# Attention and two expert layers on one core: blocks of 512 tokens, first batch in plain fp32, other planner costs

## The chip, the cores and the metric

One core of a Trainium2 chip. The metric is the device time of one execution in microseconds; lower is better.

## The reference

Attention over 4 batches of 8 heads with 576 positions of width 64, where only scores within `tau` of a row's maximum count, and then two layers, each a product up to width 2048, an activation and a product back, over the 2304 tokens of width 512, all in fp32:

```python
scores = scale * np.matmul(q, k.transpose(0, 1, 3, 2))
thresh = np.max(scores, axis=-1, keepdims=True) - tau
scores = np.where(scores >= thresh, scores, -1000000000.0)
attn = softmax(scores)
x = np.matmul(attn, v)            # then transposed to (2304, 512)
...
h = x @ w_in                      # (512, 2048)
g = np.where(h > 0.0, h, np.exp(np.minimum(h, 0.0)) - 1.0)
x = g @ w_out                     # (2048, 512)
...
h = x @ w_in2
g = np.maximum(0.01 * h, h)
out = g @ w_out2
```

## The kernel before

**Number format.** A product of two fp32 matrices is made of three products in the faster fp32r format (line 630, `passes`): high by high, high by low, low by high parts. Splitting a matrix into its parts takes a rounding copy (`copy` on ScalarE or `hi_of`) and a subtraction (`tt`). [...]

**Attention.** A unit is 128 query rows by 576 keys; 9 units make a pair of heads, 36 a batch, 144 all. In `unit` (line 423) TensorE forms the scores, for heads below `Q32` in plain fp32 from 64 partitions (`qk32`, line 456), for the others from split parts (`qk`, line 463); VectorE takes the maximum (line 475), VectorE or GpSimd adds the threshold (478, 480), ScalarE masks (484) and exponentiates (487), VectorE inverts the sum (489), GpSimd or ScalarE normalizes (490), TensorE transposes (499, 514). `weights` (520) copies the transposed weights out of PSUM: for heads below `P32` with plain copies on ScalarE only (534, 536), for the others as split parts. `pv32` (575) and `pv` (593) form the product with v. `head` (377) loads a head's k, q and v; for heads from `Q32` on, GpSimd splits k and q in four instructions (410 to 415) after two DMAs for each of k and q (404 to 409); for heads below it one DMA each (394, 395).

**Layers beside the attention.** The layers work hidden tile by hidden tile, 128 of the 2048 at a time: `step_h` (633) forms h and its activation, and two steps later (`LAG`) `step_y` (676) adds the tile's part to y in PSUM. A step has 12 matmuls of each. While the attention goes on, six blocks of `TA` = 256 tokens do the first 8 of 16 hidden tiles of layer 1; the partial y goes to memory (`evac_a`, 723). The weights are read as 64-bit numbers and turned to fp32 in seven instructions on several engines (`weight`, 249).

**Past the attention**, from about 484 us on, blocks of `TB` = 384 tokens: two finish the first 8 tiles of layer 1 for the tokens left, six do the other 8 tiles of layer 1 (`evac_b`, 743, adds the partial y), six do the 16 tiles of layer 2 (`evac_c`, 753, writes the output in four DMAs a block). h has two PSUM banks, y four.

**The order of the work.** `Order` (88) plays the whole kernel through before it is emitted: each operation has a list of engines it may run on, a duration, dependencies and a due time `vt`; whichever engine is free first takes the operation that is due first, and each engine's program is the order that comes out (108 to 176). On the chip each engine then runs its program strictly in that order. The durations are formulas (179 to 208), such as a matmul of n columns and a DMA issue on SP (60 ns, as in line 255); due times come from the unit's number times `TU` and from offsets per step (`KN`, `ST0`, `ST1`, lines 42 to 48).

Of the kernel before, what the change touches and what calls it, by code (L numbers as in the profile page):

```python
# [20 lines left out]
NH = B * H  # L21
NU = 9
# [3 lines left out]
KC = DM // 128  # L26
FC = DFF // 128
FH = FC // 2
TA, TB = 256, 384
NB = NT // TB  # L30
# [14 lines left out]
ST0 = dict(qk=3991.2, max=-10812.2, thr=3582.6, exp=-4547.6, mask=9303.1, rec=4415.0, norm=-40669.8, tr=-20834.8,  # L45
           hi=-16434.5, lo=-12049.7, lhi=-1872.6, llo=30507.0, pv=-26126.1)
ST1 = dict(qk=-8436.2, max=5560.8, thr=-5954.0, exp=-1392.3, mask=-1204.3, rec=3126.6, norm=3036.1, tr=1924.8,
           hi=-17963.2, lo=-6188.5, lhi=-3977.0, llo=993.8, pv=-5778.3)
PE, ACT, DVE, POOL, SP, HOST = "PE", "ACT", "DVE", "POOL", "SP", "HOST"

# [37 lines left out]
class Order:  # L88
# [19 lines left out]
    def run(self):  # L108
# [9 lines left out]
        free = dict.fromkeys(engines, 0.0)  # L118
# [84 lines left out]
def mm(n):  # L203
    return 3 + n / 2.4
# [7 lines left out]
def attn_moe_kernel(ctx, tc, qT, kT, vm, tau, w1i, w1o, w2i, w2o, yp, out):  # L212
# [145 lines left out]

    op((PE, 2200 + 1450 * KN["warm"], warm), [], [wps], -1e6)

    heads = {}

    def load_tau(vt):
# [9 lines left out]
        ld = op((SP, 60, lambda: nc.sync.dma_start(out=taut, in_=tau.partition_broadcast(128))), [], [], vt - 2e4,  # L373
# [3 lines left out]
    def head(g, u):  # L377
        vt = (u - KN["hleadb" if g % 2 else "hlead"]) * TU
        par = g % 2
        if g < P32:  # L380
            v = v_r.new(F32)
            ov = op((SP, 60, lambda: nc.sync.dma_start(out=v()[:, :, 0:D], in_=vm[g])), [], [v], vt + KN["vlate"],
                    lat=3000)
        else:
            vr, v = vraw_r.new(), v_r.new()
            hi, lo = (lambda: v()[:, :, 0:D]), (lambda: v()[:, :, D:2 * D])
            lv = op((SP, 60, lambda: nc.sync.dma_start(out=vr(), in_=vm[g])), [], [vr], vt - 3000, lat=3000)
# [3 lines left out]
        if g < Q32:  # L391
            k, q = k1_r.new(F32), k2_r.new(F32)
            due = vt - (3e3 if g else 3e4)
            lk = op((SP, 60, lambda: nc.sync.dma_start(out=k()[0:64], in_=kT[g])), [], [k], due, lat=3000)
            lq = op((SP, 60, lambda: nc.sync.dma_start(out=q()[0:64, 0:S], in_=qT[g])), [], [q], due, lat=3000)
# [12 lines left out]
        lk = op((SP, 120, lambda: load2(kr, kT)), [], [kr], vt - 3000, lat=3000)  # L408
        lq = op((SP, 120, lambda: load2(qr, qT)), [], [qr], vt - 3000, lat=3000)
# [333 lines left out]
    def evac_b(i, tb, ybank, ysl, last, xc, vt):  # L743
        ys = ysb[i]
        x1[i] = []
        for m in range(KC):
            yg = ybank[m][0]
            o = op((DVE, dve(TB), lambda m=m, yg=yg: nc.vector.tensor_tensor(
                out=x[:, m, i * TB:(i + 1) * TB], in0=yg(), in1=ys[0]()[:, m, :], op=ALU.add)),
                [last[m], ys[1], xc[m][2]], [yg, ys[0]], vt)  # L750
            x1[i].append([o])

    def evac_c(i, tb, ybank, ysl, last, xc, vt):
        for m in range(KC):
            yg = ybank[m][0]
            dst = x[:, m, i * TB:(i + 1) * TB]
            o = op([(ACT, actp(TB), lambda yg=yg, dst=dst: nc.scalar.copy(out=dst, in_=yg())),
                    (DVE, dve(TB), lambda yg=yg, dst=dst: nc.vector.tensor_copy(dst, yg()))],
                   [last[m], xc[m][2]], [yg], vt)
            op((SP, 60, lambda m=m, dst=dst: nc.sync.dma_start(  # L760
                out=out[m * 128:(m + 1) * 128, i * TB:(i + 1) * TB], in_=dst)), [o], [], vt, lat=2000)
# [18 lines left out]
    def block_deps(i, tb):  # L780
        b0, b1 = i * tb // S, ((i + 1) * tb - 1) // S
# [18 lines left out]
    DT = 24 * mm(TB)  # L800
# [8 lines left out]
    TT = TE + len(rest) * FH * DT  # L809
    for i in range(NB):  # L810
        vt0 = TT + i * FH * DT
        ys = ys_r.new()
        ysb[i] = (ys, op((SP, 60, lambda ys=ys, i=i: nc.sync.dma_start(out=ys(), in_=yp[:, :, i * TB:(i + 1) * TB])),
                         [o for (lo, hi), o in ypdone.items() if lo < (i + 1) * TB and hi > i * TB], [ys], vt0,
                         lat=4000))
        block(0, i, list(range(FH, FC)), TB, block_deps(i, TB)[0], hps_b, yps_b, evac_b, vt0, DT)
    T2 = TT + NB * FH * DT
# [53 lines left out]
```

## Time and profile before

| | us |
|---|---|
| median of 3 runs | 1154.95 |
| lowest, highest | 1151.43, 1155.05 |
| the profiled execution | 1155.41 |
| its span, first to last instruction | 1153.6 |
| TensorE busy (share of the span) | 1110.1 (96%) |
| VectorE, ScalarE, GpSimd busy | 706.3, 684.9, 437.7 |
| mean granted clock of TensorE | 0.984 |

PE is TensorE's matmuls, PEld its weight loads, DVE VectorE, ACT ScalarE, POOL GpSimd, SP the engine that issues all DMAs. L686 is line 686 of the kernel. A matmul's own duration has its modelled end in it, and so busy times of PE overlap; the chain of waits counts from one release to the next. The granted clock is a share of 2.4 GHz: 1.00 is that, 0.50 is 1.2 GHz.

### The profile page before, as it was taken

To read this page: it belongs to the slowest core of one execution; us is meant where nothing else is said; L and a number is where in the kernel's file an instruction comes from. 1 tells how busy PE (TensorE), PEld (TensorE's weight loads), DVE (VectorE), ACT (ScalarE), POOL (GpSimd) and SP (SyncE) were. 2 spreads that over 40 slices of the span, in tenths; PEclk is the share of its full clock that TensorE was granted. 3 is DMA by queue.
4 is the path that set the end of the run, shared out by engine and by line. 5 is a ranking of instruction groups with operands and counts; after the bars stand their busy time and mean duration, and the time that the engine had idled before them with its cause. 6 is when DMAs were issued, how large, how long until landed. Compare 5 with 4: busy or idle time off the path is not lost.

```text
span 1153.6 us, 18990 instructions
## 1 busy us (share of the span) xinstructions
PE 1110.1 (96%) x6888; PEld 1045.8 (91%) x6888; DVE 706.3 (61%) x1629; ACT 684.9 (59%) x1488; POOL 437.7 (38%) x544
## 2 busy tenths in 40 slices
PE   6988889999999999999999999999999999999998
PEld 3555469998999999999999999999999999999998
DVE  3555678877888888688988744884323233232322
ACT  4899998999999999655555533553323232232321
POOL 4577588888889978422222100120000000000000
PEclk7899899999999999999999999999999999999999
DMA  6343312122222212134543300430000000000000
GB/s 153 88 124 109 93 56 56 52 77 74 62 69 61 74 56 65 38 96 133 165 137 119 119 14 20 132 111 19 28 1 28 1 1 28 1 28 1 28 1 28
DMA packets 39437, 73.47 MB, mean 64 GB/s; under 512 B 10033, under 2 KB 23217, under 8 KB 39345
## 3 DMA queue, kind: packets, MB, share of 16 engines
q1 hardware_dynamic: 39344, 72.27, 21.2%
q8 instruction: 54, 0.88, 0.3%
q14 instruction: 39, 0.31, 0.1%
HBM read 62.82 MB, written 9.44 MB: 63 GB/s over the span
## 4 chain that ended last, share of the span: by engine, by line
PE 73%; ACT 14%; DVE 6%; POOL 3%; issue 2%; DMA 1%; SPq 0%; POOLq 0%; ACTq 0%; DVEq 0%
PE y L686 32%; PE h L645 17%; PE hb L645 14%; ACT e L487 4%; ACT ss L484 3%; PE t L499 2%; PE v L604 2%; PE s L467 2%; ACT wh L544 2%; PE v L585 2%; DVE ss L475 2%; ACT e L304 1%; DVE wl L547 1%; DVE tm L567 1%; ACT wh L566 1%
## 5 line engine op out<-in xcount | busy, mean ns | idle before, releaser
L686 PE MATMUL y<-gh,woh 128*128 128x384 f32 (+1 forms) x832 | 270.1, 325 | 0.8 <-DVE ys L567 0.8
L686 PE MATMUL y<-gl,woh 128*128 128x384 f32 (+1 forms) x832 | 268.0, 322 | 0.0
L686 PE MATMUL y<-gh,wol 128*128 128x384 f32 (+1 forms) x832 | 267.9, 322 | 0.0
L645 PE MATMUL h<-xh,wih 128*128 128x384 f32 (+1 forms) x512 | 165.6, 324 | 0.8 <-DVE g L663 0.7
L645 PE MATMUL h<-xh,wil 128*128 128x384 f32 (+1 forms) x512 | 161.0, 314 | 0.0
L645 PE MATMUL h<-xl,wih 128*128 128x384 f32 (+1 forms) x512 | 161.0, 314 | 0.0
L686 PEld LDWEIGHTS y<-gh,woh 128*128 128x128 f32 x832 | 156.6, 188 | 1.0 <-DVE ys L567 1.0
L686 PEld LDWEIGHTS y<-gl,woh 128*128 128x128 f32 x832 | 156.6, 188 | 0.1
L686 PEld LDWEIGHTS y<-gh,wol 128*128 128x128 f32 x832 | 156.6, 188 | 0.0
L670 ACT CAST gh<-g 128x384 fp32r<-128x384 f32 (+1 forms) x208 | 101.6, 489 | 90.3 <-DVE g L668 49.6
L298 POOL TENSOR_TENSOR xl<-x,xh 128x256 fp32r<-128x256 f32 (+1 forms) x35 | 30.1, 875 | 280.3 <-ACT xh L623 280.0
L297 DVE TENSOR_TENSOR gl<-g,gh 128x384 fp32r<-128x384 f32 x151 | 86.5, 574 | 57.4 <-ACT gh L670 57.3
L475 DVE TENSOR_SCALAR_CACHE_REDUCE ss<-s,scl 128x576 f32<-128x576 f32 x124 | 100.5, 811 | 22.8 <-ACT e L487 17.5
L484 ACT ACTIVATE ss<-ss,thr 128x576 f32<-128x576 f32 x144 | 111.1, 775 | 3.6 <-POOL thr L478 2.1
L487 ACT ACTIVATE e<-ss,taun 128x577 f32<-128x577 f32 x144 | 112.0, 778 | 0.8
L467 PE MATMUL s<-k,qt 128*128 128x288 f32 x528 | 97.3, 306 | 11.0 <-DVE ss L475 6.7
L645 PE MATMUL hb<-xh,wih 128*128 128x384 f32 x320 | 106.9, 334 | 0.0
L645 PE MATMUL hb<-xl,wih 128*128 128x384 f32 x320 | 106.9, 334 | 0.0
L645 PE MATMUL hb<-xh,wil 128*128 128x384 f32 x320 | 106.9, 334 | 0.0
L645 PEld LDWEIGHTS h<-xh,wih 128*128 128x128 f32 x512 | 96.8, 189 | 2.2 <-DVE g L663 2.1
L499 PE MATMUL t<-ident,e 128*128 128x128 f32 x576 | 90.1, 281 | 7.1 <-ACT e L304 3.8
L645 PEld LDWEIGHTS h<-xl,wih 128*128 128x128 f32 x512 | 96.6, 189 | 0.0
(536 smaller groups left out, 2204.2 us busy)
## 6 DMA issues: line engine op xcount, KB each, us to landing
kraw<-in_kT_dram SPq DMA_DIRECT2D x60, 160.0 KB, 2.9
qraw<-in_qT_dram SPq DMA_DIRECT2D x60, 144.0 KB, 2.8
wraw<-in_w1i_dram SPq DMA_DIRECT2D x16, 512.0 KB, 3.7
wraw<-in_w1o_dram SPq DMA_DIRECT2D x16, 512.0 KB, 3.7
wraw<-in_w2i_dram SPq DMA_DIRECT2D x16, 512.0 KB, 3.6
wraw<-in_w2o_dram SPq DMA_DIRECT2D x16, 512.0 KB, 3.6
ys<-yp_dram SPq DMA_DIRECT2D x6, 768.0 KB, 4.7
out_dram<-x SPq DMA_DIRECT2D x24, 192.0 KB, 1.9
```

The lines of the kernel that those rows point to most:

```text
L297: return pick(who, D=(dve(n), lambda: nc.vector.tensor_tensor(**args()), PORT), P=(pool_tt(n), lambda: nc.gpsimd.tensor_tensor(**args())))
L298: P=(pool_tt(n), lambda: nc.gpsimd.tensor_tensor(**args())))
L467: nc.tensor.matmul(s()[:, j, 0:HALF], q()[:, c:c + 128], kk()[:, k0 + j * HALF:k0 + (j + 1) * HALF], start=(n == 0 and m == 0), stop=(n == ...
L475: o = op((DVE, dve(S) + 60, lambda: nc.vector.tensor_scalar(out=ssr().rearrange("p (j c) -> p j c", j=2), in0=s()[:, :, 0:HALF], scalar1=s ...
L484: o = op((ACT, act(S) + 95, lambda: nc.scalar.activation(out=ssr(), in_=ssr(), func=AF.Prelu, bias=thr(), scale=-1.0, alpha=STEEP)), [ot], ...
L487: o = op((ACT, act(S) + 190, lambda: nc.scalar.activation(out=er(S + 1), in_=ssr(S + 1), func=AF.Exp, bias=taun, accum_out=su())), [o], [s ...
L499: nc.tensor.transpose(t4()[:, c, :], er()[:, c1 + c * 128:c1 + (c + 1) * 128], ident)
L544: nc.scalar.copy(out=wh()[:, :, dst], in_=t4()[:, :, src])
L585: nc.tensor.matmul(ps()[0:64, 0:nw], lhs, rhs, start=(c == 0), stop=(c == 4))
L645: nc.tensor.matmul(hp(), w_()[:, cs], x_()[:, 0:tb], start=(k == 0 and z == 0), stop=(k == KC - 1 and z == 2))
L670: o1 = op((ACT, act(tb), lambda: nc.scalar.copy(out=gh()[:, cs], in_=g()[:, cs])), [o], [g, gh], vt)
L686: nc.tensor.matmul(ysl(yg, m), w_()[:, cs], g_()[:, 0:tb], start=(first and z == 0 and share == 0), stop=(last and z == 2 and end))
```

## The change

`TB` becomes 512. The blocks past the attention are no longer numbered but listed by their first token and length: four of 512 and one of 256 (for the tokens left by the attention stage: one of 512 and one of 256). `Q32` goes from 2 to 8, so that all heads of the first batch have k and q in plain fp32. The copies of transposed weights of heads below `P32` may go to ScalarE or VectorE. The planner takes 600 ns for a DMA issue on SP (1200 for a pair), 13.3 ns instead of 3 ns as a matmul's fixed part, and a time at which each engine begins. The due times are other numbers. The DMA scratch area in SBUF shrinks to 1024 bytes.

```diff
-TA, TB = 256, 384
-NB = NT // TB
+TA, TB = 256, 512
+BLOCKS = [(a, min(TB, NT - a)) for a in range(0, NT, TB)]
...
-Q32, P32 = 2, 9
+P32, Q32 = 9, 8
...
-KN = dict(warm=3, TU=2767.5, hlead=1.68307, hleadb=3.8618, wv0=2.81039, wv1=2.45697, yoff=29757.8, coff=-4793.0,
-          NS=41, vlate=3019.0, bs=[46.53, 62.85, 80.6, 98.984, 114.51, 129.21], bdt=1.99144, look=0.0937904)
+KN = dict(warm=3, TU=2691.9, hlead=0.875114, hleadb=3.14713, wv0=3.2304, wv1=2.45697, yoff=28639.7, coff=-5493.3,
+          NS=41, vlate=-1134.2, bs=[46.53, 62.85, 80.6, 98.984, 114.51, 134.31], bdt=1.98186, look=0.0900086)
...
+BEGIN = {PE: 2100.0, ACT: 2000.0, DVE: 2400.0, POOL: 1300.0, SP: 700.0}
...
-        free = dict.fromkeys(engines, 0.0)
+        free = {e: BEGIN.get(e, 0.0) for e in engines}
...
 def mm(n):
-    return 3 + n / 2.4
+    return 13.3 + n / 2.4
...
-        ld = op((SP, 60, lambda: nc.sync.dma_start(out=raw().rearrange("p c w -> p (c w)"), in_=src.bitcast(U32))),
+        ld = op((SP, 600, lambda: nc.sync.dma_start(out=raw().rearrange("p c w -> p (c w)"), in_=src.bitcast(U32))),
...
-    op((PE, 2200 + 1450 * KN["warm"], warm), [], [wps], -1e6)
+    op((PE, 1430 * KN["warm"], warm), [], [wps], -1e6)
...
-        lk = op((SP, 120, lambda: load2(kr, kT)), [], [kr], vt - 3000, lat=3000)
+        lk = op((SP, 1200, lambda: load2(kr, kT)), [], [kr], vt - 3000, lat=3000)
...
             if f32:
-                o1 = op(copy_of("A", 4 * n, lambda wh=wh, dst=dst: wh()[:, :, dst],
+                o1 = op(copy_of("AD", 4 * n, lambda wh=wh, dst=dst: wh()[:, :, dst],
                                 lambda src=src: t4()[:, :, src]), [ott], [t, wh], vt)
-                o3 = op(copy_of("A", n, lambda lt=lt, dst=dst: lt()[64:128, dst],
+                o3 = op(copy_of("AD", n, lambda lt=lt, dst=dst: lt()[64:128, dst],
                                 lambda src=src: lv()[l0:l0 + 64, src]), [otl], [lv, lt], vt)
...
-    rest = list(range(len(beside) * TA // TB, NB))
-    for n, i in enumerate(rest):
-        deps, _ = block_deps(i, TB)
-        block(0, i, list(range(FH)), TB, deps, hps_b, yps_b, evac_a, TE + n * FH * DT, DT)
+    vt = TE
+    for t0, tb in BLOCKS:
+        if t0 >= len(beside) * TA:
+            block(0, t0, list(range(FH)), tb, block_deps(t0, tb)[0], hps_b, yps_b, evac_a, vt, dt(tb))
+            vt += FH * dt(tb)
...
-    for i in range(NB):
-        block(1, i, list(range(FC)), TB, x1[i], hps_b, yps_b, evac_c, T2 + i * FC * DT, DT)
+    for t0, tb in BLOCKS:
+        block(1, t0, list(range(FC)), tb, x1[t0], hps_b, yps_b, evac_c, vt, dt(tb))
+        vt += FC * dt(tb)
...
-    nc = _bacc.Bacc("TRN2", target_bir_lowering=False, num_devices=1)
+    nc = _bacc.Bacc("TRN2", target_bir_lowering=False, num_devices=1, dynamic_dma_scratch_size=1024)
```

## Rows read from the trace of the kernel before

**Rows 1.** Windows: PE, PEld, DVE, ACT, POOL busy us (x count), clock, DMA share, GB/s.

```profile
36.00:168.00 132.00, 111.64 (x567) 70.56 (x566) 79.73 (x220) 125.43 (x267) 95.20 (x103) 0.96 0.35 96
168.00:484.00 316.00, 307.12 (x2419) 296.31 (x2420) 261.40 (x720) 292.66 (x707) 263.69 (x352) 1.00 0.21 59
484.00:1150.00 666.00, 665.99 (x3843) 665.67 (x3842) 350.47 (x646) 250.00 (x486) 63.16 (x69) 1.00 0.17 54
```

**Rows 2.** The chain of waits: start us, us, what; products are on L604, L645, L686.

```profile
88.70 2.46 PE v L585 x10
...
474.13 1.31 PE v L604 x9
475.45 1.44 PE h L645 x12
476.88 0.44 PE t L499 x4
...
490.63 2.08 PE y L686 x12
...
1148.46 2.12 DVE x L758 x4
```

**Rows 3.** Windows of line 484, the mask, one per unit: ScalarE's busy us (x masks).

```profile
36.00:140.00 104.00, 24.40 (x32) 0.95 0.39 107
```

**Rows 4.** Groups of ScalarE, 36 to 168 us: count | busy us, mean ns | idle before.

```profile
L566 ACT COPY wh<-t 128x512 f32<-128x512 f32 x33 | 19.3, 586 | 4.0 <-PE t L499 3.5
L304 ACT ACTIVATE e<-e,rs 128x576 f32<-128x576 f32 x22 | 17.0, 771 | 0.3 <-DVE rs L489 0.2
L566 ACT COPY lt<-h 64x128 f32<-64x128 f32 x34 | 8.8, 260 | 1.0 <-PE h L514 0.3
```

**Rows 5.** Groups of the whole span: VectorE's copy of 128x512 out of PSUM.

```profile
L567 DVE COPY ys<-y 128x512 f32<-128x512 f32 x7 | 4.8, 692 | 2.7 <-PE y L686 2.5
```

**Rows 6.** Windows of GpSimd's instructions on kraw (first row) and qraw (second).

```profile
36.00:168.00 132.00, 20.41 (x18) 0.96 0.35 96
...
36.00:168.00 132.00, 17.37 (x16) 0.96 0.35 96
```

**Rows 7.** TensorE's timeline at full clock: start us, us, engine, line, operation.

```profile
35.77 1.23 PE L460 MATMUL y<-k,k 64*128 64x288 f32 x4
36.93 0.66 PE L499 MATMUL t<-ident,e 128*128 128x128 f32 x4
...
106.31 2.37 PE L585 MATMUL v<-wh,v 128*64 128x320 f32 x8 [0.98 <-ACT wh L566]
...
109.29 0.66 PE L499 MATMUL t<-ident,e 128*128 128x128 f32 x4
...
110.43 0.69 PE L467 MATMUL y<-k,qt 128*128 128x288 f32 x4
110.96 0.60 PE L499 MATMUL t<-ident,e 128*128 128x128 f32 x4
```

**Rows 8.** The timeline of the start; in brackets the idle time and its releaser.

```profile
6.33 1.23 PE L460 MATMUL s<-k,k 64*128 64x288 f32 x4
...
10.97 0.69 DVE L280 CUSTOM_DVE_ANT_0 wb__144<-wb__144,wa__136 128x1024 uint16<-128x1024 uint16 x1 [0.73 <-ACT wa__136 L278]
...
11.58 0.81 DVE L475 TENSOR_SCALAR_CACHE_REDUCE ss<-s,scl 128x576 f32<-128x576 f32 x1
...
12.45 2.28 PE L460 MATMUL s<-k,k 64*128 64x288 f32 x4 [3.92 <-DVE ss L475]
...
17.19 0.67 POOL L302 TENSOR_SCALAR qt<-qraw 128x576 fp32r<-128x576 f32 x1 [3.53 <-DMA qraw<-in_qT_dram]
17.84 0.27 POOL L478 TENSOR_SCALAR thr<-nm,taup 128x1 f32<-128x1 f32 x1
...
18.14 1.44 ACT L484 ACTIVATE ss<-ss,thr 128x576 f32<-128x576 f32 x2 [2.06 <-POOL thr L478]
```

**Rows 9.** Windows of 4 us in the first batch, columns as in rows 1.

```profile
28.00:32.00 4.00, 4.00 (x11) 2.23 (x10) 1.49 (x4) 2.20 (x5) 2.13 (x4) 0.50 0.55 152
```

More of the change, by code (lines that the diff above doesn't have):

```diff
@@ L38 @@
 U0 = H // 2 * NU
-Q32, P32 = 2, 9
-KN = dict(warm=3, TU=2767.5, hlead=1.68307, hleadb=3.8618, wv0=2.81039, wv1=2.45697, yoff=29757.8, coff=-4793.0,
-          NS=41, vlate=3019.0, bs=[46.53, 62.85, 80.6, 98.984, 114.51, 129.21], bdt=1.99144, look=0.0937904)
[L45 to L48, printed above, removed]
+KN = dict(warm=3, TU=2691.9, hlead=0.875114, hleadb=3.14713, wv0=3.2304, wv1=2.45697, yoff=28639.7, coff=-5493.3,
+          NS=41, vlate=-1134.2, bs=[46.53, 62.85, 80.6, 98.984, 114.51, 134.31], bdt=1.98186, look=0.0900086)
+ST0 = dict(qk=-9654.3, max=10644.8, thr=2482.6, exp=2393.0, mask=12204.5, rec=6620.5, norm=-37112.7, tr=-9608.6,
+           hi=-42015.3, lo=-19519.3, lhi=5300.4, llo=36737.3, pv=-43029.6)
+ST1 = dict(qk=-9964.6, max=12029.4, thr=-7385.7, exp=-1635.0, mask=-3627.9, rec=-3292.6, norm=5228.6, tr=1657.3,
+           hi=-7831.6, lo=-13359.9, lhi=-853.3, llo=-2960.2, pv=-4125.4)
 PE, ACT, DVE, POOL, SP, HOST = "PE", "ACT", "DVE", "POOL", "SP", "HOST"
+BEGIN = {PE: 2100.0, ACT: 2000.0, DVE: 2400.0, POOL: 1300.0, SP: 700.0}
 HOPS = {
@@ L371, in taus @@
                                     op0=ALU.is_ge, op1=ALU.mult)
-        ld = op((SP, 60, lambda: nc.sync.dma_start(out=taut, in_=tau.partition_broadcast(128))), [], [], vt - 2e4,
+        ld = op((SP, 600, lambda: nc.sync.dma_start(out=taut, in_=tau.partition_broadcast(128))), [], [], vt - 2e4,
                 lat=2000)
@@ L381, in head @@
             v = v_r.new(F32)
-            ov = op((SP, 60, lambda: nc.sync.dma_start(out=v()[:, :, 0:D], in_=vm[g])), [], [v], vt + KN["vlate"],
+            ov = op((SP, 600, lambda: nc.sync.dma_start(out=v()[:, :, 0:D], in_=vm[g])), [], [v], vt + KN["vlate"],
                     lat=3000)
@@ L386, in head @@
             hi, lo = (lambda: v()[:, :, 0:D]), (lambda: v()[:, :, D:2 * D])
-            lv = op((SP, 60, lambda: nc.sync.dma_start(out=vr(), in_=vm[g])), [], [vr], vt - 3000, lat=3000)
+            lv = op((SP, 600, lambda: nc.sync.dma_start(out=vr(), in_=vm[g])), [], [vr], vt - 3000, lat=3000)
             o5 = op(hi_of("P", 320, hi, vr), [lv], [vr, v], vt + 1)
@@ L393, in head @@
             due = vt - (3e3 if g else 3e4)
-            lk = op((SP, 60, lambda: nc.sync.dma_start(out=k()[0:64], in_=kT[g])), [], [k], due, lat=3000)
-            lq = op((SP, 60, lambda: nc.sync.dma_start(out=q()[0:64, 0:S], in_=qT[g])), [], [q], due, lat=3000)
+            lk = op((SP, 600, lambda: nc.sync.dma_start(out=k()[0:64], in_=kT[g])), [], [k], due, lat=3000)
+            lq = op((SP, 600, lambda: nc.sync.dma_start(out=q()[0:64, 0:S], in_=qT[g])), [], [q], due, lat=3000)
             heads[g] = (k, k, q, v, (lk, lq), ov)
@@ L614, in pv, with conv_x @@
         xready.setdefault((bt, hp), []).append(o)
-    def conv_x(i, tb, deps, vt, reg):
+    def conv_x(t0, tb, deps, vt, reg):
         res = []
@@ L621, in conv_x @@
             xh, xl = xh_r[k].new(), xl_r[k].new()
-            src = x[:, k, i * tb:(i + 1) * tb]
+            src = x[:, k, t0:t0 + tb]
             o = op((ACT, act(tb), lambda xh=xh, src=src: nc.scalar.copy(out=xh()[:, 0:tb], in_=src)),
@@ L694, in attn_moe_kernel, with block @@
     ypdone = {}
-    def block(layer, i, fs, tb, deps, hps, yrings, evac, vt0, dt, reg=False):
-        xc = conv_x(i, tb, deps, vt0 - dt + (KN["coff"] if reg else 0), reg)
+    def block(layer, t0, fs, tb, deps, hps, yrings, evac, vt0, dt, reg=False):
+        xc = conv_x(t0, tb, deps, vt0 - dt + (KN["coff"] if reg else 0), reg)
         ybank = ysl = None
@@ L710, in ysl @@
             def ysl(yg, m):
-                return yg()
+                return yg()[:, 0:tb]
         for n in range(len(fs) + LAG):
@@ L720, in block, with evac_a @@
                     lasty[m].append(res[m])
-        evac(i, tb, ybank, ysl, [lasty[m][-1] for m in range(KC)], xc, vt0 + (len(fs) + LAG) * dt - 2 * dt)
-    def evac_a(i, tb, ybank, ysl, last, xc, vt):
+        evac(t0, tb, ybank, ysl, [lasty[m][-1] for m in range(KC)], xc, vt0 + (len(fs) + LAG) * dt - 2 * dt)
+    def evac_a(t0, tb, ybank, ysl, last, xc, vt):
         ys = ys_r.new()
         done = []
-        if tb == TA:
+        if ybank[0][0] is ybank[1][0]:
             yg = ybank[0][0]
@@ L734, in evac_a, with evac_b, evac_c @@
                 yg = ybank[m][0]
-                done.append(op(copy_of("AD", tb, lambda m=m: ys()[:, m, 0:tb], lambda yg=yg: yg()),
+                done.append(op(copy_of("AD", tb, lambda m=m: ys()[:, m, 0:tb], lambda yg=yg: yg()[:, 0:tb]),
                                [last[m]], [yg, ys], vt))
-        ypdone[i * tb, (i + 1) * tb] = op(
-            (SP, 60, lambda: nc.sync.dma_start(out=yp[:, :, i * tb:(i + 1) * tb], in_=ys()[:, :, 0:tb])),
+        ypdone[t0, t0 + tb] = op(
+            (SP, 600, lambda: nc.sync.dma_start(out=yp[:, :, t0:t0 + tb], in_=ys()[:, :, 0:tb])),
             done, [ys], vt, lat=4000)
     x1 = {}
-    def evac_b(i, tb, ybank, ysl, last, xc, vt):
-        ys = ysb[i]
-        x1[i] = []
+    def evac_b(t0, tb, ybank, ysl, last, xc, vt):
+        ys = ysb[t0]
+        x1[t0] = []
         for m in range(KC):
             yg = ybank[m][0]
-            o = op((DVE, dve(TB), lambda m=m, yg=yg: nc.vector.tensor_tensor(
-                out=x[:, m, i * TB:(i + 1) * TB], in0=yg(), in1=ys[0]()[:, m, :], op=ALU.add)),
+            o = op((DVE, dve(tb), lambda m=m, yg=yg: nc.vector.tensor_tensor(
+                out=x[:, m, t0:t0 + tb], in0=yg()[:, 0:tb], in1=ys[0]()[:, m, 0:tb], op=ALU.add)),
                 [last[m], ys[1], xc[m][2]], [yg, ys[0]], vt)
-            x1[i].append([o])
-    def evac_c(i, tb, ybank, ysl, last, xc, vt):
+            x1[t0].append([o])
+    def evac_c(t0, tb, ybank, ysl, last, xc, vt):
         for m in range(KC):
             yg = ybank[m][0]
[L756 to L761, printed above, removed]
+            dst = x[:, m, t0:t0 + tb]
+            o = op(copy_of("AD", tb, lambda dst=dst: dst, lambda yg=yg: yg()[:, 0:tb]), [last[m], xc[m][2]], [yg], vt)
+            op((SP, 600, lambda m=m, dst=dst: nc.sync.dma_start(
+                out=out[m * 128:(m + 1) * 128, t0:t0 + tb], in_=dst)), [o], [], vt, lat=2000)
     NUN = NH // 2 * NU
@@ L778, in close_attn, with block_deps @@
         late["psb"] = ctx.enter_context(tc.tile_pool(name="psb", bufs=1, space=PSUM))
-    def block_deps(i, tb):
-        b0, b1 = i * tb // S, ((i + 1) * tb - 1) // S
+    def block_deps(t0, tb):
+        b0, b1 = t0 // S, (t0 + tb - 1) // S
         return [sum((xready[b_, k] for b_ in range(b0, b1 + 1)), []) for k in range(KC)], b1
@@ L785, in attn_moe_kernel @@
     for i in beside:
-        deps, bt = block_deps(i, TA)
+        deps, bt = block_deps(i * TA, TA)
         vt0, dt = KN["bs"][i] * TU, KN["bdt"] * TU
-        block(0, i, list(range(FH)), TA, deps, hps_a, yps_a, evac_a, vt0, dt, reg=True)
+        block(0, i * TA, list(range(FH)), TA, deps, hps_a, yps_a, evac_a, vt0, dt, reg=True)
     banks = itertools.cycle([lambda: psm.tile([128, 512], F32, tag="h", name="h", bufs=1),
@@ L798, in attn_moe_kernel, with dt @@
         op((HOST, 0, gen), d, [gen], 0)
-    DT = 24 * mm(TB)
+    def dt(tb):
+        return 24 * mm(tb)
     ysb = {}
@@ L804, in attn_moe_kernel @@
             weight(0, which, f, TE + (2 * (f - FH) + j) * 3.5e3, after=[end_a])
-    rest = list(range(len(beside) * TA // TB, NB))
-    for n, i in enumerate(rest):
-        deps, _ = block_deps(i, TB)
-        block(0, i, list(range(FH)), TB, deps, hps_b, yps_b, evac_a, TE + n * FH * DT, DT)
-    TT = TE + len(rest) * FH * DT
-    for i in range(NB):
-        vt0 = TT + i * FH * DT
-        ys = ys_r.new()
[L813 to L817, printed above, removed]
+    vt = TE
[3 more added lines that the diff above has]
+            vt += FH * dt(tb)
+    TT = vt
+    for t0, tb in BLOCKS:
+        ys = ys_r.new()
+        ysb[t0] = (ys, op((SP, 600, lambda ys=ys, t0=t0, tb=tb: nc.sync.dma_start(
+            out=ys()[:, :, 0:tb], in_=yp[:, :, t0:t0 + tb])),
+            [o for (lo, hi), o in ypdone.items() if lo < t0 + tb and hi > t0], [ys], vt, lat=4000))
+        block(0, t0, list(range(FH, FC)), tb, block_deps(t0, tb)[0], hps_b, yps_b, evac_b, vt, dt(tb))
+        vt += FH * dt(tb)
+    T2 = vt
     for f in range(FH):
@@ L822, in attn_moe_kernel @@
         for j, which in enumerate(("wi", "wo")):
-            weight(1, which, f, T2 - FH * DT + (f - FH + j * LAG) * DT)
-    for i in range(NB):
-        block(1, i, list(range(FC)), TB, x1[i], hps_b, yps_b, evac_c, T2 + i * FC * DT, DT)
+            weight(1, which, f, T2 - FH * dt(BLOCKS[-1][1]) + (f - FH + j * LAG) * dt(TB))
+    for t0, tb in BLOCKS:
+        block(1, t0, list(range(FC)), tb, x1[t0], hps_b, yps_b, evac_c, vt, dt(tb))
+        vt += FC * dt(tb)
     with tc.manual_schedule():
```

2 lines of the change are left out of this document (1 added, 1 removed).

## The prediction

> **What bounds the kernel now.** I read the windows by stage first, since a mean over the span mixes three limits. From 484 us to the end [rows 1] TensorE is busy in 665.99 of 666 us with nothing but products of the two layers: that stretch is as long as its matmuls. From 168 to 484 us TensorE is busy for 307 of 316 us, with attention units and the first blocks of 256 tokens between them; at most 9 us lie there. From 36 to 168 us it is ScalarE that is full (125.4 of 132 us), while VectorE stands at 80, GpSimd at 95 and TensorE at 112, whose busy time counts the modelled ends. So a gain lies in the price of a matmul after 484 us, and in what ScalarE does, and when it starts, before 168 us.
>
> In the chain of waits twelve matmuls of 384 columns take 2.08 us, 173.3 ns each, and twelve of 256 take 1.44 us, 119.8 ns each [rows 2]. The difference over 128 columns is 0.418 ns a column, which leaves about 13 ns that each matmul costs whatever its width.
>
> **Blocks of 512.** Before, 2 blocks do 8 of the hidden tiles, 6 blocks the other 8, and 6 blocks 16 in the second layer: 160 steps of 24 matmuls, 3840, as the window counts (x3843) [rows 1]. After, each stage has blocks of 512 and one of 256: 1+4 blocks of 8 steps and 4 of 16 make 104 steps at 512, 1+1 of 8 and 1 of 16 make 32 at 256: 2496 + 768 = 3264 matmuls. No row has such a product of 512 columns. By the line through 256 and 384 it costs 173.3 + 128 x 0.418 = 226.8 ns. So 2496 x 226.8 + 768 x 119.8 = 658.1 us against 3840 x 173.3 = 665.5: **-7.4 us**. Ends: nine products of 320 columns take 1.31 us, 145.6 ns [rows 2]; the slope from 256 to 320 gives 224.9 ns at 512 and -12 us, plain proportion from 384 gives 231.1 ns and +3 us. I take the middle because the two rows nearest in kind (layer products, 256 and 384) make it. The conversions and activations of a block stay beside TensorE: a step grows from 4.16 us to 5.44, and VectorE and ScalarE had 350 and 250 us of work in 666 [rows 1]. In the 256 block a step is 2.87 us and the product that needs an activation comes two steps later; VectorE's work per column hardly changes, so I charge nothing; if that cover is gone, one block's boundary shows, 1 to 2 us.
>
> The Trainium skill (TensorE: Matmul & The Clock Gate, "Wait — 56ns, not 53.3ns?") puts the fixed part of a warm matmul at about 2.5 ns, downstream of decode. By that figure 576 fewer matmuls would bring about 1.5 us (an estimate from the page), not 7.4. The two rows disagree with it here: 13 ns.
>
> **The end.** The last block's four copies start at 1148.46 us on VectorE, 2.12 us together [rows 2]. At 256 columns each is shorter, but four DMA issues follow one another either way: 0, within 0.3 us. The smaller DMA scratch meets no transfer of this kernel (all are issued by SP): 0.
>
> **Copies on either engine.** Between 36 and 168 us ScalarE copies transposed weights out of PSUM 33 times at 586 ns and 34 times at 260 ns, 28 us in all, and normalizes 22 times at 771 ns, 17 us [rows 4]. On VectorE a copy of 128x512 takes 692 ns [rows 5]; with its 80 us of work it has room for half of them (14 us become some 17).
>
> **Heads 2 to 7 in plain fp32 (Q32 = 8).** This takes from GpSimd the splitting of k and q: 20.4 us for 9 heads' k and 17.4 us for 8 heads' q [rows 6], 2.3 + 2.2 = 4.4 us a head, 27 us for six heads, and one of the two DMAs of each load. GpSimd can then take more of ScalarE's normalizing. By both edits ScalarE's 125 us could fall to some 100 (14 from copies, about 11 from norms). The price is on TensorE: a unit's four products of q and k take 0.53 us split (110.43 to 110.96) and 1.16 us in fp32 (35.77 to 36.93) [rows 7]. A pair of heads has 9 units, of which one has double the products. After: 10 x 1.16; nine times four transposes at 0.44; five small transposes, about 0.15 each by the same row; and for each of two heads ten value products of 256 columns at 2.46 [rows 2] and ten of 320 at 2.98 (106.31 to 109.29) [rows 7]: 11.6 + 4.0 + 0.8 + 10.9 = 27.3 us, **3.03 us a unit**, where it was 21.0 us, 2.33 a unit.
>
> That is what decides the stretch. Masks, one per unit, count the pace: 32 in the 104 us from 36 to 140, 3.25 us a unit [rows 3]. ScalarE set 3.25; with 100 of its 125 us left it would allow 2.6, but TensorE now allows 3.03 at best. At 97% filling, 3.13, the 27 units of the three changed pairs win 27 x 0.12 = **-3 us**. Ends: -6 with TensorE full, +9 if both engines hinder each other and it fills only 85% (3.57).
>
> **The start.** Unit 0's products begin at 6.33 us and last 1.23, but VectorE takes its maximum at 11.58, behind a weight's conversion that ran from 10.97; the first mask runs at 18.14, because a threshold on GpSimd (17.84) stands behind the first piece of a q split that waited for its DMA until 17.19 [rows 8]. The planner had thought that a DMA issue takes 60 ns and that engines start at 0; with 600 ns and the begin times, the raw weight comes later in its plan and the maximum goes first; and with Q32 = 8 no q split stands on GpSimd's queue before the fifth pair. Products done at 7.6, 0.8 for the maximum as at 11.58, 0.2 for the threshold, hops: the mask could run at 9.2 to 9.6, **-8.5 us**. Ends: 0, if other work is put ahead; -14, if the cold stretch also goes: at 28 to 32 us TensorE is busy throughout at a granted clock of 0.50 [rows 9], after a pause of 3.92 us to 12.45, which ends with the late maximum [rows 8].
>
> **From 168 to 484 us** the order is a new one, by corrected costs of products, but TensorE's work is the same: 0, from -4 to +5.
>
> **Sum.** The profiled execution took 1155.4 us (span 1153.6), 0.5 above the median of the runs, 1154.95. 1155.4 - 7.4 - 3 - 8.5 = 1136.5, **1137**. A measurement tells about 0.3% (3.5 us) from no change.
>
> **Rivals.**
> *An even exchange.* TensorE takes ScalarE's place in the first batch at the old pace, the gained start is used up waiting, and only the blocks count: 1155.4 - 7.4 = 1148. For it: 3.03 is near 3.25, and ScalarE's copies are taken by whichever engine the plan thinks free, perhaps ScalarE again. Against it: the late start has two causes, and both go. Chance 0.22.
> *The clock falls in the first batch: slower.* With three more pairs in fp32 on half of the array's rows, TensorE could run at the lower of its two levels, 1.2 GHz, as it does at 28 to 32 us [rows 9]. The three pairs hold 82 us of TensorE work; a share s at half clock costs 82 x s. Gains of 19 us are lost at s = 0.23, and 0.27 is slower by more than the bound. At s = 0.4, a little more than half way to the lasting 0.50, 1137 + 33 = 1170. Against it: the window of 36 to 168 us reads 0.96 [rows 1], and fuller work leaves fewer pauses. Chance 0.08.
> *A matmul's price goes by columns.* The blocks bring 0 and the rest stays: 1144. The 256 row speaks against it. The skill's small fixed cost, named above, lies near this rival. Chance 0.07.
> *The change goes further:* the start gives 14 and TensorE is full, 1128; this is the low end of the forecast.
>
> **How the numbers follow.** Forecast 0.63, own range 1126 to 1147. The low end 1124 takes the unknown prices on their good side, the high end 1151 the even exchange with some loss; left out are the slower case and a few hundredths on each side. Faster by over 0.3%: nearly all of the forecast and of the column rival, most of the even exchange, 0.86; within: 0.07; slower: 0.07.
>
> **What would show it.** Right: twelve matmuls of 512 in 2.72 us in the chain, about 658 us from the first to the last; a first mask near 9.5 us; the first layer block, now from about 168 us on, some 11 us earlier; TensorE in place of ScalarE as the full engine from 20 to 140 us; copies of 128x512 on VectorE there. Wrong: 2.77 us for the twelve; a mean granted clock under 0.9 between 36 and 140 us; masks still 3.25 us apart or more; new waits of TensorE for block conversions after 484 us.

## The result, and the profile after

The changed kernel takes **1142.82 us** (median of five runs, 1140.93 to 1146.65), where the kernel before took 1154.95 beside it. The ratio is 0.9908, with a 95% interval of 0.9885 to 0.9931: faster, by 8 to 13 us. The forecast was 1137 with a range of 1124 to 1151; the result lies inside the range, and the middle is 6 us too low. The profiled execution took 1140.95 us (span 1139.2), 1.9 below the median.

The windows of the changed kernel by stage, that is the first batch, the middle stage beside the first layer blocks, and the last stretch (columns as in [rows 1]):

```profile
36.00:168.00 132.00, 126.62 (x651) 80.76 (x650) 105.05 (x288) 114.80 (x241) 84.02 (x105) 0.97 0.28 83
168.00:472.80 304.80, 292.42 (x2270) 279.57 (x2268) 252.23 (x683) 280.24 (x667) 245.75 (x325) 1.00 0.21 61
472.80:1135.30 662.50, 661.58 (x3288) 563.59 (x3288) 341.79 (x598) 246.47 (x442) 31.31 (x33) 1.00 0.17 54
```

Beside [rows 1]: in the first batch TensorE has taken ScalarE's place as the full engine (126.6 of 132 us, it was 111.6), and VectorE works 25 us more. The stretch of nothing but layer products begins at 472.9 in place of 484.2 us and is 3.5 us shorter. In the middle TensorE now leaves 12.4 us of 304.8 unused, where it left 8.9 of 316.

The chain of waits around the beginning of the last stretch, and in it (start us, us, what):

```profile
472.88 3.01 PE h L647 x12
475.89 2.72 PE hb L647 x12
478.61 2.72 PE h L647 x12
481.33 2.72 PE y L688 x12
...
740.69 2.87 PE y L688 x24
```

Twelve matmuls of 512 columns take 2.72 us, 226.7 ns each; the line through 256 and 384 [rows 2] had given 226.8. The last row is a step of 24 matmuls in a block of 256 tokens, 119.6 ns each.

The timeline of the changed kernel's start (in brackets idle time and releaser), which answers to [rows 8]:

```profile
8.71 0.82 DVE L477 TENSOR_SCALAR_CACHE_REDUCE ss<-s,scl 128x576 f32<-128x576 f32 x1 [3.12 <-PE s L462]
...
9.57 0.21 DVE L482 TENSOR_SCALAR thr<-nm,taup 128x1 f32<-128x1 f32 x1
...
9.81 0.78 ACT L486 ACTIVATE ss<-ss,thr 128x576 f32<-128x576 f32 x1 [1.56 <-DVE thr L482]
...
12.48 0.67 POOL L304 TENSOR_SCALAR qt<-qraw 128x576 fp32r<-128x576 f32 x1 [0.16 <-DMA qraw<-in_qT_dram]
...
18.04 0.67 POOL L304 TENSOR_SCALAR qt<-qraw 128x576 fp32r<-128x576 f32 x1 [0.82 <-DMA qraw<-in_qT_dram]
```

The first mask runs at 9.81 us, where it ran at 18.14. The maximum goes first on VectorE and the threshold stands on VectorE too. But GpSimd still splits q at 12.48 and 18.04 us, for later heads: the splits did not leave its queue, they only no longer stand ahead of anything urgent.

The groups of the changed kernel from 36 to 168 us that answer to [rows 4] (ScalarE), and VectorE's new copies:

```profile
L306 ACT ACTIVATE e<-e,rs 128x576 f32<-128x576 f32 x18 | 13.8, 769 | 1.1 <-DVE rs L491 1.0
L568 ACT COPY wh<-t 128x512 f32<-128x512 f32 x18 | 10.5, 582 | 5.8 <-PE t L501 5.6
...
L569 DVE COPY wh<-t 128x512 f32<-128x512 f32 x13 | 8.9, 687 | 1.1 <-PE t L501 0.8
...
L569 DVE COPY lt<-h 64x128 f32<-64x128 f32 x21 | 6.1, 289 | 1.3 <-PE h L516 0.9
```

ScalarE's 33 copies of 128x512 have become 18; 13 now run on VectorE, at 687 ns each (692 in [rows 5]). ScalarE now waits longer for TensorE's transposes ahead of its copies (5.6 us, it was 3.5). With three more masks in the window than before (45 for 42) ScalarE still has 11 us less work.

### The profile page after: what moved, and what is told of

Read it like the earlier page. It is cut to its first block, busy times and chain, and to the rows that moved or that the text cites. A ratio compares the mean times of both kernels' runs of the same rounds, so it can differ in the third digit from the quotient of the medians.

```text
span 1139.2 us, 17486 instructions
## 1 busy us (share of the span) xinstructions
PE 1112.0 (98%) x6312; PEld 940.5 (83%) x6312; DVE 721.1 (63%) x1633; ACT 665.1 (58%) x1391; POOL 375.9 (33%) x485
## 4 chain that ended last, share of the span: by engine, by line
PE 76%; ACT 11%; DVE 9%; issue 2%; POOL 1%; POOLq 0%; DVEq 0%; ACTq 0%
PE y L688 31%; PE h L647 16%; PE hb L647 14%; PE v L587 4%; ACT e L489 3%; PE t L501 3%; ACT ss L486 3%; DVE ss L477 2%; PE s L469 2%; ACT wh L546 2%; PE v L606 2%; PE s L462 1%; PE y L462 1%; DVE wl L549 1%; DVE g L659 1%
## 5 line engine op out<-in xcount | busy, mean ns | idle before, releaser
L688 PE MATMUL y<-gh,woh 128*128 128x512 f32 (+1 forms) x736 | 256.8, 349 | 1.6 <-ACT ys L568 1.6
L688 PE MATMUL y<-gl,woh 128*128 128x512 f32 (+1 forms) x736 | 252.3, 343 | 0.0
L688 PE MATMUL y<-gh,wol 128*128 128x512 f32 (+1 forms) x736 | 252.1, 343 | 0.0
L647 PE MATMUL h<-xh,wih 128*128 128x256 f32 (+1 forms) x464 | 157.1, 338 | 3.9 <-DVE g L665 3.6
L647 PE MATMUL h<-xl,wih 128*128 128x256 f32 (+1 forms) x464 | 153.2, 330 | 0.0
L647 PE MATMUL h<-xh,wil 128*128 128x256 f32 (+1 forms) x464 | 153.1, 330 | 0.0
L688 PEld LDWEIGHTS y<-gl,woh 128*128 128x128 f32 x736 | 139.3, 189 | 16.2
L688 PEld LDWEIGHTS y<-gh,wol 128*128 128x128 f32 x736 | 139.0, 189 | 16.2
L672 ACT CAST gh<-g 128x512 fp32r<-128x512 f32 (+1 forms) x184 | 97.1, 528 | 86.2 <-DVE g L670 46.9
L647 PEld LDWEIGHTS h<-xh,wih 128*128 128x128 f32 x464 | 88.1, 190 | 14.4 <-DVE g L665 3.7
L647 PE MATMUL hb<-xl,wih 128*128 128x512 f32 (+1 forms) x272 | 99.1, 364 | 0.0
L647 PE MATMUL hb<-xh,wih 128*128 128x512 f32 (+1 forms) x272 | 99.0, 364 | 0.0
L647 PE MATMUL hb<-xh,wil 128*128 128x512 f32 (+1 forms) x272 | 99.0, 364 | 0.0
```

Source lines behind the costliest of these rows:

```text
L647: nc.tensor.matmul(hp(), w_()[:, cs], x_()[:, 0:tb], start=(k == 0 and z == 0), stop=(k == KC - 1 and z == 2))
L672: o1 = op((ACT, act(tb), lambda: nc.scalar.copy(out=gh()[:, cs], in_=g()[:, cs])), [o], [g, gh], vt)
L688: nc.tensor.matmul(ysl(yg, m), w_()[:, cs], g_()[:, 0:tb], start=(first and z == 0 and share == 0), stop=(last and z == 2 and end))
```

## The experiments

The question was which of the parts makes the 12 us, and what became of the 8.3 us by which the first mask is earlier. Every kernel was timed in five rounds, beside the kernel before (medians 1154.2 to 1154.8). "Old plan" stands for the planner's durations and due times of before.

**The blocks alone.** The kernel before with only this (and, with it, the code that goes through the list of blocks, and the smaller DMA scratch):

```diff
-TA, TB = 256, 384
-NB = NT // TB
+TA, TB = 256, 512
+BLOCKS = [(a, min(TB, NT - a)) for a in range(0, NT, TB)]
```

> Only the blocks of 512 tokens are added to the kernel before; order costs, due times, Q32 = 2 and ScalarE's copies stay. If a matmul has a fixed part of 13 ns and nothing else changes past the attention: 7 us faster than before, ratio 0.9936, and the twelve products of 512 columns at 2.72 us. If a matmul's price goes by its columns: ratio 1.000. The first mask stays near 18 us in both cases.

Measured 1148.54 us, ratio 0.9953 (0.9937 to 0.9968): -5.7, with an interval of -3.7 to -7.3. A group and the window of its last stretch (group: count | busy us, mean ns | idle before; window as in [rows 1]):

```profile
L688 PE MATMUL y<-gl,woh 128*128 128x512 f32 x416 | 162.0, 389 | 1.2 <-DVE gl L299 1.2
```

```profile
483.70:1144.00 660.30, 659.05 (x3269) 561.06 (x3268) 349.98 (x592) 228.31 (x414) 71.15 (x70) 1.00 0.17 54
```

TensorE is busy for 659.05 us with 3269 products; the forecast of 658.1 was for 3264, and five of 256 columns that the window still catches from the stage before make 0.6. A wait of 1.2 us for a conversion (gl) takes back a part of what the price brought. (The mean of 389 ns is the time of one matmul in a pipeline; the step from one to the next is the 226.7 ns of the chain.)

**The plan alone.** The changed kernel with blocks, heads and copies of before:

```diff
-P32, Q32 = 9, 8
+P32, Q32 = 9, 2
-TA, TB = 256, 512
+TA, TB = 256, 384
-copy_of("AD", 4 * n, lambda wh=wh
+copy_of("A", 4 * n, lambda wh=wh
-copy_of("AD", n, lambda lt=lt
+copy_of("A", n, lambda lt=lt
```

> Only the planner's costs, begin times and due times are new; blocks of 384, Q32 = 2, copies on ScalarE. If the late start came from the plan: first mask at 9 to 11 us and 5 to 9 us faster than before, ratio 0.992 to 0.996. If it came from the q splits on GpSimd's queue, which Q32 = 8 takes away: first mask still near 18 us, ratio 0.998 to 1.005. ScalarE is full from the start to 165 us in both.

Measured 1157.91 us, ratio 1.0038 (1.0025 to 1.0051): slower, by 3 to 6 us. Its first mask runs at 10.21 us. So the early start comes from the plan and not from the heads in fp32, and the plan by itself brings nothing.

**The heads undone, the copies undone.** The changed kernel with Q32 = 2 alone, and with the two "A" lines above alone:

> The changed kernel with Q32 back at 2. If plain fp32 for heads 2 to 7 wins by freeing GpSimd and ScalarE: 3 to 8 us slower than the changed kernel (1146 to 1151). If TensorE's dearer products cost as much as they free (even exchange): 1141 to 1145. If they cost more: faster than the changed kernel, 1135 to 1140.

> The changed kernel with the first batch's copies back on ScalarE alone. If the choice of engine relieves ScalarE, which was the full engine: 3 to 9 us slower than the changed kernel (1146 to 1152), with ScalarE again over 93% busy from 36 to 140 us. If TensorE is the bound there now and ScalarE has room enough: within 2 us of 1143.

Measured 1152.59 us (0.9993, 0.9980 to 1.0006) with two heads in plain fp32 (k and q not split), first mask 8.86; and 1144.05 (0.9915, 0.9899 to 0.9931) with the copies on ScalarE, first mask 8.68. Under the new plan the heads carry 9.8 us, more than the 3 to 8 expected. The copies carry 1.2, which these runs can't tell from 0, although without them ScalarE is nearly full again (window of that kernel, columns as in [rows 1]):

```profile
36.00:140.00 104.00, 99.34 (x460) 55.71 (x458) 65.34 (x186) 100.72 (x216) 62.38 (x74) 1.00 0.31 92
```

The granted clock here is 1.00, where the changed kernel has 0.97 in the same window (shown below). So part of what the copies bring may be lost to the clock; no run separates the two.

**The plan undone.** The changed kernel with the old plan, blocks, heads and copies kept (the two tables of due times, ST0 and ST1, go back with it):

```diff
-KN = dict(warm=3, TU=2691.9, hlead=0.875114, ...
+KN = dict(warm=3, TU=2767.5, hlead=1.68307, ...
-BEGIN = {PE: 2100.0, ACT: 2000.0, DVE: 2400.0, POOL: 1300.0, SP: 700.0}
+BEGIN = {}
-    return 13.3 + n / 2.4
+    return 3 + n / 2.4
-    op((PE, 1430 * KN["warm"], warm), [], [wps], -1e6)
+    op((PE, 2200 + 1450 * KN["warm"], warm), [], [wps], -1e6)
-(SP, 600,
+(SP, 60,
-(SP, 1200,
+(SP, 120,
```

> The changed kernel with the planner's costs, begin times and due times all as before; blocks of 512, Q32 = 8 and copies on either engine stay. If the new plan loses again between 168 and 484 us what it wins at the start (as it seemed with the plan alone, 4 us slower than before): 1136 to 1143, not slower than the changed kernel, with fewer than 8 masks by 36 us. If costs and times only suit Q32 = 8 and are worth what they were tuned for: 4 to 12 us slower than the changed kernel, 1147 to 1155.

> The version with blocks of 512, six more heads in fp32 and the copies on either engine, under the old plan, once more beside the two others, since it was 2.7 us below the changed kernel and that is less than 0.3%. If it is the faster one, 1138 to 1142 again, an interval of its ratio to the kernel before wholly below 0.990; if that was the luck of one chip, 1142 to 1145.

Measured 1140.13 us (0.9875, 0.9858 to 0.9893), and the second time 1139.08 (0.9860, 0.9840 to 0.9881). It beats both kernels: its medians lie 2.7 and 3.7 us below the changed kernel's. The first interval (to 0.9893) still overlaps the changed kernel's (from 0.9885), the second (to 0.9881) does not. Its first mask runs at 17.2 and 18.2 us, as late as before. Windows of line 486, the mask, in its second run and in the changed kernel (ScalarE's busy us, masks, clock):

```profile
0.00:36.00 36.00, 4.52 (x6) 0.72 0.53 146
36.00:140.00 104.00, 27.00 (x36) 1.00 0.31 90
```

```profile
0.00:36.00 36.00, 6.92 (x9) 0.91 0.58 157
36.00:140.00 104.00, 26.14 (x34) 0.97 0.31 90
```

The late starter does 36 units in the 104 us, the early one 34, and before it was 32 [rows 3].

**Heads without copies under the old plan.** The version just told, with the two "A" lines:

> The kernel before with blocks of 512 and with six more heads in plain fp32 (Q32 = 8), copies on ScalarE alone, old plan: the blocks alone gave 1148.5, these two with the copies 1140.1. If fp32 for six heads is the part that shortens the first batch whatever the plan, 1139 to 1143, with a first mask near 17 us and 33 or more masks between 36 and 140 us. If the heads need the copies (VectorE taking them from ScalarE) to gain under this plan, 1145 to 1149 and ScalarE fuller than 97 of 104 us between 36 and 140 us.

Measured 1145.29 us (0.9915, 0.9896 to 0.9933). So under the old plan the heads bring 3.2 us by the medians (1148.5 to 1145.3) and the copies 5 to 6 (to 1140.1 and 1139.1). By the ratios it is 4.4 and 4.6 to 6.4. Either way the heads bring less and the copies more than under the new plan, though for the copies the intervals leave some doubt. It is the second reading that holds, with ScalarE at 99 of 104 us. The window of 36 to 140 us without and with the copies (columns as in [rows 1]):

```profile
36.00:140.00 104.00, 99.13 (x455) 55.85 (x455) 62.19 (x179) 99.25 (x211) 56.52 (x69) 1.00 0.31 89
```

```profile
36.00:140.00 104.00, 100.70 (x469) 56.88 (x467) 85.08 (x220) 91.26 (x186) 59.72 (x74) 1.00 0.31 90
```

Without the copies ScalarE and TensorE are both full; with them VectorE carries 23 us more and TensorE alone is full.

**Durations against due times.** The changed kernel with the old durations only, with the old due times only, and with part of them (the first batch's times new, the later ones old); and with the last block beside the attention due where it was before (bs ending in 129.21 for 134.31):

> The changed kernel with the old costs (60 ns a DMA issue, 3 ns a matmul's fixed part, engines beginning at 0) under the new due times. If the first mask came early because of the costs: it is at 14 us or later and the kernel 3 to 8 us slower than the changed one. If the due times did it: first mask near 10 us and within 3 us of the changed kernel.

> The changed kernel with the planner's new durations and begin times but every due time of before: the fourth of the combinations of old and new durations with old and new due times. If an early start is kept to the end, the new durations alone bring a first mask near 10 us and some 7 us less than the 1140.1 of old durations and old times: 1132 to 1136. If the start is given back whichever way it comes, the first mask is near 10 us and the time 1139 to 1146. If durations and due times only fit together, as the 1146.9 of old durations with new times says, it is above 1145.

> The changed kernel with the unit length and the due times of the later three batches and of the blocks beside them as before; the first batch's times and all costs stay new. If these late due times are what gives the lead of 20 us at 168 us back: 3 to 9 us faster than the changed kernel (1134 to 1140). If the loss between 168 and 484 us comes with any order in which the attention leads: within 2 us. If they were tuned to the new costs: slower by 3 us or more.

> The changed kernel with one number changed: the last block beside the attention is due at 129.21 units, as before, instead of 134.31. If the end of the overlapped stage is slow because the attention ends first and the last block is left alone with one bank for h: 2 to 4 us faster than the changed kernel. If not: within 1.5 us of it.

With blocks, heads and copies in all of them:

```
                    old due times     new due times
old durations       1140.1, 1139.1    1146.9 (0.9917 to 0.9949)
new durations       1150.6            1142.8 (0.9885 to 0.9931)
                    (0.9949 to 0.9981)
```

The part with old later times gave 1144.59 (0.9896 to 0.9928), the last block's old time 1140.93 (0.9870 to 0.9910): neither can be told from the changed kernel, so it is not shown that what is given back hangs on those times or on that block. Among these four, durations and due times fit in pairs; mixed, they cost 7 to 11 us against the old pair and 4 to 8 against the new. The first mask runs at 14.3 us with old durations under new due times, and at 10.1 with new durations under the old: it is the durations and begin times that make most of the early start.

**The start alone.** The best version, and of the new plan only the engines' begin times (with the warm-up's duration that goes with them) and the 600 ns of a DMA issue:

```diff
-BEGIN = {}
+BEGIN = {PE: 2100.0, ACT: 2000.0, DVE: 2400.0, POOL: 1300.0, SP: 700.0}
-    op((PE, 2200 + 1450 * KN["warm"], warm), [], [wps], -1e6)
+    op((PE, 1430 * KN["warm"], warm), [], [wps], -1e6)
-(SP, 60,
+(SP, 600,
-(SP, 120,
+(SP, 1200,
```

> The version of 1139 (blocks of 512, six more heads in fp32, copies on either engine, old plan), and of the planner's corrections the begin times and the 600 ns of a DMA issue alone; the price of a product and every due time stay the old ones. This is the start by itself. If what the start gains is kept, the first mask comes near 10 us in place of 18.2 and the time is 7 to 9 us less, 1130 to 1133. If the start is given back in the later order, whichever plan it is joined to, first mask near 10 us, 8 or 9 masks by 36 us, and 1137 to 1145.

Measured 1140.78 us (0.9880, 0.9859 to 0.9900). Its first mask, and its masks in the two windows:

```profile
9.16 0.76 ACT L486 ACTIVATE ss<-ss,thr 128x576 f32<-128x576 f32 x1
```

```profile
0.00:36.00 36.00, 6.79 (x9) 0.81 0.61 159
36.00:140.00 104.00, 24.51 (x32) 0.97 0.30 87
```

Nine microseconds at the first mask, and no time gained at the end. By 140 us it has 41 masks, where the late starter has 42: here the lead is gone within the first batch. It differs from the 1150.6 version only in the product's price (3 or 13.3 ns ahead of the columns), so under the old due times that truer price alone costs some 10 us. (The price also enters the due times of the blocks past the attention, which are set 24 products apart.)

## Why the prediction was right, and where its steps failed

**The blocks (-7.4): right in price, 1.7 too much in all.** The chain shows 2.72 us for twelve, the stretch of the blocks alone 659.05 us of products. I had charged nothing for a block's boundary and named 1 to 2 us if its cover is gone; 1.2 is there. The rival by columns would have given none, and falls. The Trainium skill (TensorE: Matmul & The Clock Gate, "Wait — 56ns, not 53.3ns?") has a fixed part of about 2.5 ns for warm matmuls back to back; the trace disagrees, with 13 ns up to 512 columns.

**The first batch (-3): the right pace, for too few units.** From the timelines of ScalarE, the start of the 9th, 36th and 45th mask (a pair of heads has nine units; a mask can be one of a row of two), before:

```profile
48.07 0.78 ACT L484 ACTIVATE ss<-ss,thr 128x576 f32<-128x576 f32 x1
...
136.62 1.44 ACT L484 ACTIVATE ss<-ss,thr 128x576 f32<-128x576 f32 x2
...
161.56 0.79 ACT L484 ACTIVATE ss<-ss,thr 128x576 f32<-128x576 f32 x1
```

for the version with the old plan (in the first row it is the second of the two):

```profile
40.23 1.57 ACT L486 ACTIVATE ss<-ss,thr 128x576 f32<-128x576 f32 x2
...
126.14 0.78 ACT L486 ACTIVATE ss<-ss,thr 128x576 f32<-128x576 f32 x1
...
149.17 0.79 ACT L486 ACTIVATE ss<-ss,thr 128x576 f32<-128x576 f32 x1
```

and for the changed kernel:

```profile
34.61 0.76 ACT L486 ACTIVATE ss<-ss,thr 128x576 f32<-128x576 f32 x1
...
121.40 0.78 ACT L486 ACTIVATE ss<-ss,thr 128x576 f32<-128x576 f32 x1 [1.18 <-POOL thr L480]
...
143.47 0.79 ACT L486 ACTIVATE ss<-ss,thr 128x576 f32<-128x576 f32 x1
```

With the heads alone under the old plan (copies on ScalarE) they start at 47.11, 131.30 and 156.11 us. So:

```
us per stretch   before   heads alone,   heads and copies,   changed
of units                  old plan       old plan
first mask       18.1     18.6           18.2                 9.8
1st to 9th       29.9     28.5           22.8                24.8
9th to 36th      88.6     84.2           85.1                86.8
36th to 45th     24.9     24.8           23.0                22.1
```

The three pairs that go to fp32 run at 3.15 us a unit under the old plan and 3.21 in the changed kernel, and I had said 3.13. They win 3.5 and 1.8 us, and I had said 3. What I left out are the two pairs around them: 7.1 and 1.9 us under the old plan, 5.1 and 2.8 in the changed kernel. Their products don't change. Under the old plan most of this comes with the copies: the heads alone win 1.4 and 0.1 there. In the changed kernel that holds for the first pair only: with the copies back on ScalarE it takes 29.5 us, but the fifth still 22.3, and what shortens the fifth stays open. Nor do the parts add up there: plan_only, with neither heads nor copies, takes 24.6 for the first. (The masks of neighbouring pairs mix: if the stretches are cut one mask later, the outer pairs win 3.4 and 2.6 us under the old plan and the three 5.7.) So the step that failed is "the 27 units of the three changed pairs": the copies relieve ScalarE, the full engine, in units whose products nobody changed. In the total, heads and copies bring 8.4 to 9.5 us under the old plan (1148.5 to 1140.1 and 1139.1).

**The start (-8.5): the event right, its worth wrong.** The mask came at 9.81, forecast 9.2 to 9.6. Of my two causes one holds, the maximum ahead of the weight's conversion; the other, that no q split stands on GpSimd before the fifth pair, is false (12.48, 18.04 us above), and the run with Q32 = 2 has its first mask at 8.86 all the same. The low end's "-14, if the cold stretch also goes" came in part too: the granted clock from 0 to 36 us is 0.91 (above), where before it is 0.67. But the 8.5 was put into the sum as kept to the end, and two runs show that it isn't: the start alone makes 1140.8 of 1139.1 to 1140.1, and plan_only is slower than before. That part of the even exchange ("the gained start is used up waiting") was right in that the gain is used up, and only in part by waiting; its other part, that the first batch wins nothing, was wrong.

**From 168 to 484 us (0, from -4 to +5): wrong, some 8 us given back.** I count TensorE's products done by 168 us against before, at the mean step from one start to the next that they have in this stage before, without idle time (busy times overlap and would count too much). The changed kernel has 57 more of the layers (0.129 us each), 20 more of values (0.138), 24 of q and k fewer left (0.141) and 27 more transposes (about 0.10): 16 us ahead. Its first layer product comes at 142.7 us, where it came at 159.4; the forecast had some 11 us. At the end of the stage it is 8.2: 484.2 - 472.9, less 24 products of 256 columns left over (3.1). The version with the old plan is 10.9 ahead by the same count and keeps 10.1; the start alone is 12.2 ahead and keeps 8.7. TensorE's waits from 168 to 476 us (us in total, times, longest us), first before, then the old plan, the changed kernel, and the start alone:

```profile
PE s L467 <- DVE ss L475: 2.7, 6, 1.1
```

```profile
PE t L516 <- DVE wl L549: 2.3, 2, 1.4
PE t L501 <- DVE wl L549: 1.5, 2, 0.9
PE h L647 <- DVE g L665: 1.1, 2, 0.9
```

```profile
PE s L469 <- DVE ss L477: 5.4, 14, 0.8
PE h L647 <- DVE g L665: 3.6, 5, 1.4
```

```profile
PE s L469 <- DVE ss L477: 4.3, 5, 1.4
PE h L647 <- DVE g L665: 2.0, 4, 0.9
```

TensorE waits for the buffer that the maximum on VectorE reads: in the changed kernel 14 times, before 6 times, with the old plan not among its longest waits. The idle time of TensorE in the stage is 12.4 us, where it was 8.9 [rows 1]: 3.5 of the 8 us. The rest are longer steps: 0.132 us for one of the 1059 layer products, 0.144 for one of the 400 of q and k, together 4.3. A product of q and k that follows a wait has a step of 0.24 us in place of 0.16, but that makes less than 1 us of it; why the other steps are longer stays open. That the due time of the maximum is what makes the waits was not tried by itself; with the later due times of before, mixed with new durations, they were still 3.9 us.

**The end (0).** From the last product to the end of the span 4.1 us, it was 3.6.

**The sum.** Forecast -7.4 - 3 - 8.5; the runs give -5.7 for the blocks, -8.4 for heads and copies, and +2.7 for the plan. The two profiles, which are 14.4 us apart (spans 1153.6 and 1139.2), say the same by stage: 16.2 us ahead at 168 us, where the forecast had 11.5; 8.0 given back by the end of the middle stage, where it had 0; 6.6 gained in the last stretch without what was left over, where it had 7.4; and 0.5 lost at the end. That the total came out only 6 us off is in part luck: a first batch that wins more than forecast hides half of a start that wins nothing in the end.

Of the rivals, the clock's did not come: 0.97 from 36 to 140 us, and 1.00 with the old plan, where before it was 0.95 [rows 3]. The forecast had said against it that fuller work leaves fewer pauses, which fits. (In its price, a share of 0.4 at half clock is somewhat less, not more, than half of the way to the lasting 0.50.)

## What to carry to other kernels

A lead at the first instruction is not a term of a sum: follow it to the border of each stage, count there the work done ahead, and ask what consumes it. Count it by the step from one product to the next, since busy times overlap. When a full engine is relieved, count every unit that runs through it, not only those that the edit names. Here a planner's corrected durations brought nothing without due times fitted to them: try each alone and both, and keep the old pair as a candidate, since here it was the best.

## What was not expected of the hardware

In the changed kernel, and in the one with the start alone, TensorE fell to its lower level a second time, well inside the first batch. Windows of 8 us (columns as in [rows 1]), of the changed kernel, then of the start alone, then of the old plan, and last of the kernel before:

```profile
48.00:56.00 8.00, 7.01 (x32) 4.29 (x31) 7.75 (x21) 7.08 (x14) 3.92 (x4) 0.94 0.35 107
56.00:64.00 8.00, 8.00 (x24) 3.88 (x23) 4.33 (x14) 4.30 (x10) 3.33 (x4) 0.63 0.36 104
```

```profile
56.00:64.00 8.00, 5.97 (x17) 2.87 (x17) 5.62 (x17) 7.98 (x18) 5.24 (x6) 0.75 0.50 162
64.00:72.00 8.00, 8.00 (x31) 3.81 (x29) 4.03 (x10) 3.91 (x8) 2.22 (x4) 0.82 0.10 24
```

```profile
56.00:64.00 8.00, 8.00 (x36) 4.45 (x36) 6.48 (x17) 6.71 (x14) 3.78 (x8) 1.00 0.36 104
```

```profile
124.00:132.00 8.00, 7.13 (x23) 3.36 (x20) 3.97 (x8) 7.25 (x17) 6.70 (x6) 0.57 0.11 46
```

In the first two TensorE had just paused (7.01 and 5.97 us busy of 8), and the mean granted clock of the window lies between its two levels of 2.4 and 1.2 GHz: for part of it TensorE ran at the lower one, also where it had no pause (8.00 of 8). In the third it had not paused and kept 1.00. From 56 to 64 us the changed kernel does 24 matmuls, the old plan 36. But an early start is neither needed for such a fall nor enough: the kernel before, which starts late, shows one in the last window, and the version with the copies back on ScalarE, whose first mask is the earliest (8.68), keeps 1.00 from 36 to 140 us.

The fall takes back a part of what the early start brings: 0.97 in place of 1.00 over 104 us is 3 us. Over the first 140 us the changed kernel still loses less to the clock than the old plan (0.91 and 0.97 against 0.72 and 1.00 in the two windows of the mask above, 6 against 10 us), while the start alone loses as much as the old plan (0.81 and 0.97, 10 us).

The five runs of the changed kernel follow their clock as well: 1140.9 and 1141.0 us at a mean granted clock of 0.994 and 0.993, 1142.8 at 0.990, 1144.5 at 0.989, 1146.7 at 0.986. The eight runs of the old plan all have 0.991 and lie between 1138.8 and 1140.9 us, so the higher clock alone does not make the changed kernel as fast.
